# Block 0 of a four-layer transformer kernel: whole V chunks, x tile 1 in halves, its transposes moved among the third chunk's products, x tile 3 loaded ahead of x tile 2

## The chip, the core and the metric

The kernel runs on one core of a Trainium2 chip. The metric is the device time of one execution in microseconds (us). Five engines work side by side: TensorE (PE, matrix products and transposes), VectorE (DVE), ScalarE (ACT), GpSimd (POOL) and SyncE (SP). Here SP only issues DMAs. ACT issues a few DMAs at the very start and then computes.

## The reference

Four layers are applied in turn to `x` of shape 1 x 2048 x 1024 (bf16). Each adds its result to `x`:

```
x = x + A(layernorm(x));  x = x + B(layernorm(x));  x = x + A(layernorm(x));  x = x + B(layernorm(x))
A: qkv = x @ wqkv; 32 heads of 32; each position attends to itself and 7 earlier positions, 2 apart;
   softmax over the 8 logits; weighted sum of v; @ wo
B: (relu(x @ W_gate) * (x @ W_up)) @ W_down        # 1024 -> 3584 -> 1024
```

The layernorm has no weights: it subtracts the row's mean and divides by the square root of the variance plus 1e-5.

## The kernel before

The 2048 positions are four blocks of 512, and each block is four tiles of 128 positions (`x_tiles[0]` to `x_tiles[3]` are block 0). All of `x` stays on the chip; weights stream through a ring of five slabs (`wring`), each of at most 1 MB.

The order on an engine is fixed when the program is built. `sp_dma` chains the DMAs that SP issues, `dv` chains VectorE's instructions, `pe_group` TensorE's, and `on("a", ...)` and `on("g", ...)` ScalarE's and GpSimd's in block 0. An instruction that waits holds up everything behind it on its engine. DMAs use eight completion semaphores in rotation. A DMA waits at its issue until the DMA eight places earlier has landed.

The change touches the first products, the V projection of block 0. `w_v` is loaded as eight chunks of 128 rows of `wqkv` by 1024 columns (256 KB each), four to a slab; `load_slab` writes them out one by one, and halves some by columns. `kc` numbers the chunks. `v_first` multiplies them: `prod(kc, t)` is two products of 128x512, one for each half of the columns, of chunk `kc` with tile `t`, into accumulators that live until `kc` = 7. `head()` is the order on TensorE, written out by hand.

Before a tile can be multiplied, it must be centred (its mean subtracted) and turned (transposed). Tiles 0 and 1 are turned on TensorE when only centred; the division by the deviation comes later, on the results (`put`, on VectorE) and on the turned tiles (`widen`). `open_up()` starts tile 0: its halves' sums (`half_sums`, one on VectorE, one on ScalarE), `centre(0)`, `turn(0)` into four PSUM tiles, four copies back to SBUF by VectorE; then tile 1's mean in one pass of ScalarE (`act_mean(1)`) and `centre(1)`. Tile 1 is turned after the products of tile 0 with chunks 0 to 2. Its transposes lie in two PSUM tiles, which VectorE and ScalarE copy. Tiles 2 and 3 are divided too before they are turned (`apply`), tile 2 by TensorE (`later`) and tile 3 by a DMA transpose (`turn_last`). Their statistics, and those of tiles 0 and 1, are made on VectorE (`bn`, `aggr`), ScalarE (`square_of`, `act_mean`) and GpSimd (`power`) while TensorE multiplies chunks 3 to 7. `spread_rstd` turns the two deviations for `widen`. Tiles 2 and 3 are then multiplied with all eight chunks, and the q and k products of block 0 follow.

Ahead of this, ten products of constants (`scratch`) keep TensorE busy until `x` is there.

Of the kernel before, what the change touches and what calls it, by code (L numbers as in the profile page):

```python
# [36 lines left out]
def kernel(  # L37
# [86 lines left out]
    def sp_dma(dst, src, transpose=False):  # L124
        start = nc.sync.dma_start_transpose if transpose else nc.sync.dma_start
        if tail_sp[0] is None:
            tail_sp[0] = start(dst, src).ins  # L127
        else:
            with tc.issue_after(tail_sp[0]):
                tail_sp[0] = start(dst, src).ins  # L130
# [49 lines left out]
    def load_x(b, tiles=range(TPB)):  # L180
        for t in (b * TPB + i for i in tiles):
            if t == 0:
                sp_dma(x_tiles[t][:, 0:SLAB], x_dram[t * P:(t + 1) * P, 0:SLAB])
                nc.scalar.dma_start(x_tiles[t][:, SLAB:D], x_dram[t * P:(t + 1) * P, SLAB:D])
            elif t == 1:
                nc.scalar.dma_start(x_tiles[t][:], x_dram[t * P:(t + 1) * P, :])
            else:
                sp_dma(x_tiles[t][:], x_dram[t * P:(t + 1) * P, :])

# [36 lines left out]
    def want_down(n, half, at, gap):  # L226
        for s in range(NSL):
            rows = slice(8 * s, min(8 * (s + 1), FC))
            want(("d", n, half, s), wd_v[:, rows, half * SLAB:(half + 1) * SLAB], at + gap * min(8 * (s + 1), FC))

    def load_slab(key, src):
        shp = list(src.shape)
        t = wring.tile([P, 8 * SLAB], BF16, tag="slab", name="w_" + "_".join(str(k) for k in key))
        tv = t[:, 0:shp[1] * shp[2]].rearrange("p (a b) -> p a b", b=shp[2])
        if key[0] == "v0":
            for i in range(KC // 2):
                if (key[1], i) == (1, 0):
                    load_x(0, [2, 3])
                width = SLAB if (key[1], i) in ((0, 2), (1, 0)) else D
                for c in range(0, D, width):  # L240
                    sp_dma(tv[:, i:i + 1, c:c + width], src[:, i:i + 1, c:c + width])
        else:
            sp_dma(tv, src)
        slab[key] = tv
# [84 lines left out]
    def ln_first():  # L329
# [4 lines left out]
        def on(eng, f, *args, **kwargs):  # L334
            if eng == "v":
                dv(f, *args, **kwargs)
            elif eng in last:
                with tc.issue_after(last[eng]):
                    last[eng] = f(*args, **kwargs).ins
            else:  # L340
                last[eng] = f(*args, **kwargs).ins

        def small(name, bufs=4):
            return stat_pool.tile([P, 1], F32, tag="f" + name, name=name, bufs=bufs)
# [24 lines left out]

        parts = {}  # L370

        def half_sums():
            parts[0] = [small("part0"), small("part1")]
            on("v", nc.vector.tensor_scalar, xna[:, 0, 0:SLAB], x_tiles[0][:, 0:SLAB], 1.0 / D, None, op0=ALU.mult,
               op1=ALU.add, accum_out=parts[0][0][:])
            on("a", nc.scalar.activation, xna[:, 0, SLAB:D], x_tiles[0][:, SLAB:D], ACT.Identity, scale=1.0 / D,
               accum_out=parts[0][1][:])

        def centre(t):
            for h in range(2):  # L380
                cols = slice(h * SLAB, (h + 1) * SLAB)
                if t == 0:
                    on("v", nc.vector.tensor_scalar, xna[:, t, cols], x_tiles[t][:, cols], parts[t][0][:],
                       parts[t][1][:], op0=ALU.subtract, op1=ALU.subtract)
                else:
                    on("v", nc.vector.tensor_scalar, xna[:, t, cols], x_tiles[t][:, cols], mean[t], None,
                       op0=ALU.subtract)

        def square_of(src, t):
            sq = small("sq1")  # L390
# [3 lines left out]
        def act_mean(t):  # L394
            mn = small("mean1")
            on("a", nc.scalar.activation, xna[:, t, :], x_tiles[t][:], ACT.Identity, scale=1.0 / D, accum_out=mn[:])
            mean[t] = mn[:]
# [29 lines left out]
        def turn(t, halves=(0, 1)):  # L427
            if t in tps:
                pass
            elif t == 0:  # L430
                tps[t] = [psum.tile([P, KC // 4, P], BF16, tag="acc", name=f"tp{h}")[:] for h in range(4)]
            else:
                tps[t] = [pool["turns"].tile([P, KC // 2, P], BF16, tag=f"half{h}", name=f"tp{h}")[:] for h in range(2)]
            for c in (h * (KC // 2) + i for h in halves for i in range(KC // 2)):
                n = KC // len(tps[t])
                with pe_group():
                    tail_pe[0] = nc.tensor.transpose(tps[t][c // n][:, c % n, :], xna[:, t, c * P:(c + 1) * P],  # L437
                                                     ident[:]).ins

        def copy(t, eng, h, parts=1):  # L440
            f = nc.vector.tensor_copy if eng == "v" else nc.scalar.copy
            n = KC // len(tps[t])
            m = n // parts
            for i in range(0, n, m):
                on(eng, f, hold["xnT"][:, t, h * n + i:h * n + i + m, :], tps[t][h][:, i:i + m, :])

        def open_up():
            warm = small("warm")
            on("a", nc.scalar.activation, warm[:], one(1), ACT.Identity)
            scratch([BLK] * 9 + [BLK // 2])  # L450
            half_sums()
            centre(0)
            turn(0)
            for h in range(4):
                copy(0, "v", h)
            act_mean(1)
            centre(1)

        hold.update(on=on, bn=bn, aggr=aggr, apply=apply, turn=turn, copy=copy, widen=widen,
# [27 lines left out]
    def v_first(ln):  # L487
        st = att[0]
        accs = {}

        def prod(kc, t, hs=(0, 1)):
            for h in hs:
                if kc == 0:
                    accs[t, h] = psum.tile([P, SLAB], F32, tag="acc", name="acc_v")
                with pe_group():
                    mm(accs[t, h][:], lhsT=ln["xnT"][:, t, kc, :],
                       rhs=slab["v0", kc // (KC // 2)][:, kc % (KC // 2), h * SLAB:(h + 1) * SLAB],
                       start=(kc == 0), stop=(kc == KC - 1))

        def put(t):  # L500
            for h in range(2):
                v = ln["xn"][:, t, h * SLAB:(h + 1) * SLAB]
                if t < 2:
                    dv(nc.vector.tensor_scalar, v, accs.pop((t, h))[:], ln["rpair"][:, t:t + 1], None, op0=ALU.mult)
                else:
                    ln["on"]("a", nc.scalar.copy, v, accs.pop((t, h))[:])

        def later(t, h):
            ln["turn"](t, (h,))
            ln["copy"](t, "a", h, 2 - h)  # L510

        def turn_last():
            sp_dma(ln["xnT"][:, TPB - 1, :, :], ln["xn"][:, TPB - 1, :], True)
            load_x(1, [1])

        def head():
            ln["open_up"]()
            for kc in range(3):
                prod(kc, 0)
            ln["turn"](1)  # L520
            ln["copy"](1, "v", 0)
            ln["copy"](1, "a", 1)
            prod(3, 0)
            for kc in range(4):
                prod(kc, 1)
            for h in range(2):
                for t in range(2):
                    prod(4, t, (h,))
            for t in range(2):
                prod(5, t)  # L530
            ln["bn"](2, 0)
            ln["bn"](2, 1)
            ln["aggr"](2)
            sq = ln["square_of"](x_tiles[3][:], 3)
            ln["act_mean"](3)
            ln["bn"](1, 0)
            ln["apply"](2)
            ln["act_power"](3, sq)
            ln["power"](0, ln["square_of"](ln["xn"][:, 0, :], 0)[:], 1.0)
            ln["bn"](1, 1)  # L540
            ln["apply"](3)
            ln["aggr"](1)
            turn_last()
            prod(6, 0)
            prod(6, 1)
            later(2, 0)
            prod(7, 0)
            put(0)
            later(2, 1)
            prod(7, 1)  # L550
            ln["spread_rstd"]()
            put(1)
            ln["widen"]()
            for t in range(2, TPB):
                for kc in range(KC):
                    prod(kc, t)
                put(t)
            tail_act[0] = ln["last"]["a"]

        return head  # L560
# [482 lines left out]
    for t, steps in enumerate(norm_at):  # L1043
        ev.extend(zip(steps, (stats[t], apply[t], turn(t))))
    spread([turn_v(t) for t in range(TPB)], t_qk0 + 19.0, 0.01)
    spread([store_v_first(c0, c1) for c0, c1 in ((0, 3), (3, 6), (6, 8))], t_qk1 + 3.4, 0.87)
    ev.append((t_qk0 + 18.0, lambda: load_x(3)))
    spread(qk_steps(0, ln_a[0], "qk01"), t_qk0, GRP)
    spread(prod_sum_steps(0), t_sum0, 4.4)
# [146 lines left out]
```

## Time and profile before

| | |
|---|---|
| median of 3 runs | 1614.24 us (1614.2 to 1614.36) |
| the profiled execution | 1614.92 us, of which span 1613.2 us |
| PE busy | 1606.4 us (100% of the span), 7444 products recorded |
| DVE, ACT, POOL busy | 1140.9, 477.3, 183.3 us |
| granted TensorE clock | 1.00 |

The span runs from the first to the last instruction that the profiler recorded; the 1.7 us between it and the execution's time lie outside. Busy time counts a product from its start to its modelled end, and the ends overlap: in a dense stretch 128x512 products start 0.216 us apart though each is shown with 0.38 us. So idle time is better read from starts than from the busy share.

When the weights and tiles of block 0 landed, from the semaphore records of the trace (the last of the 16 counts of each DMA; us from the span's start):

| DMA | issued | landed |
|---|---|---|
| tile 0, two halves (SP and ACT) | 0.81, 0.80 | 3.66, 3.49 |
| tile 1 (ACT) | 1.24 | 5.16 |
| chunks 0, 1 | 1.27, 1.75 | 5.35, 6.70 |
| chunk 2, two halves | 2.23, 2.71 | 7.09, 7.45 |
| chunk 3 | 3.19 | 8.13 |
| tiles 2, 3 | 3.66, 4.16 | 8.81, 9.51 |
| chunk 4, two halves | 5.18, 5.55 | 9.86, 10.19 |
| chunks 5, 6, 7 | 6.72, 7.11, 7.57 | 10.85, 11.49, 12.89 |

### The profile page before, as it was taken

The page shows a single profiled execution, that of the slowest core. Times are in us where ns is not written, and L with a number is a line of the kernel's source. Part 1 is how long each engine was busy: PE and PEld are TensorE (multiplying, and loading weights), DVE is VectorE, ACT ScalarE, POOL GpSimd, SP SyncE. Part 2 cuts the span into 40 slices and gives each one's busy share as a digit, 9 for nine tenths or more (in the row PEclk, how much of TensorE's full clock was granted, in tenths as well). Part 3 has the DMA queues.
Part 4 walks back from the last instruction along what each step waited for, and adds up shares of the span by engine and source line. Part 5 has one row for each costly group of instructions (what it writes and reads, how often), then busy time and mean ns, then how long its engine had stood idle before and what let it go on. Part 6 is the DMA issues. An engine that isn't in the chain of part 4 may idle for free.

```text
span 1613.2 us, 18644 instructions
## 1 busy us (share of the span) xinstructions
PE 1606.4 (100%) x7444; PEld 776.2 (48%) x7494; DVE 1140.9 (71%) x967; ACT 477.3 (30%) x976; POOL 183.3 (11%) x172
## 2 busy tenths in 40 slices
PE   9999999999999999999999999999999999999999
PEld 5646544444444445444454444544445444444444
DVE  7999979997989698929389393993939939311211
ACT  4952311131125313603136031361313311131110
POOL 3500000010002002300053000530005100000000
DMA  9897867596669666784747857488575885655452
GB/s 287 214 215 251 212 177 239 188 231 199 201 195 239 184 189 198 203 241 147 231 153 206 232 159 230 151 205 249 164 227 156 203 244 157 209 168 171 157 164 71
DMA packets 365015, 319.22 MB, mean 198 GB/s; under 512 B 110592, under 2 KB 339456, under 8 KB 364416
## 3 DMA queue, kind: packets, MB, share of 16 engines
q1 hardware_dynamic: 364352, 317.41, 67.7%
q8 instruction: 58, 0.95, 0.2%
q10 hardware_dynamic: 576, 0.62, 0.1%
q14 instruction: 29, 0.24, 0.0%
HBM read 266.29 MB, written 34.66 MB: 187 GB/s over the span
## 4 chain that ended last, share of the span: by engine, by line
PE 99%; DMA 0%; issue 0%; SPq 0%; DVE 0%
PE acc_u L141 24%; PE acc_g L141 24%; PE dacc L141 18%; PE acc_k L141 7%; PE acc_q L141 7%; PE acc_v L141 7%; PE acc_wo L141 7%; PE dacc_pair L141 6%; DMA w_v<-in_A_wqkv_dram 0%; PE tp L437 0%; PE L L141 0%; SPq L130 0%; SPq L127 0%; DVE x L947 0%
## 5 line engine op out<-in xcount | busy, mean ns | idle before, releaser
L141 PE MATMUL acc_g<-xnT_b,w_g 128*128 128x512 bf16 x1792 | 423.5, 379 | 0.0
L141 PE MATMUL acc_u<-xnT_b,w_u 128*128 128x512 bf16 x1792 | 423.4, 379 | 0.0
L895 ACT ACTIVATE r<-acc_g 128x512 bf16<-128x512 f32 x224 | 133.6, 596 | 727.7 <-PE acc_g L141 690.9
L115 DVE TENSOR_TENSOR hT<-acc_u,r 128x512 bf16<-128x512 f32 x224 | 150.7, 686 | 240.9 <-PE acc_u L141 238.2
L141 PE MATMUL dacc<-w_d,hT 128*128 128x512 bf16 (+1 forms) x1372 | 301.9, 376 | 1.5
L141 PEld LDWEIGHTS <-hT 128*128 128x128 bf16 x1820 | 176.6, 98 | 210.5
L141 PEld LDWEIGHTS <-w_u 128*128 128x128 bf16 x1792 | 175.0, 98 | 211.8
L141 PEld LDWEIGHTS <-w_g 128*128 128x128 bf16 x1792 | 175.0, 98 | 211.7
L115 DVE TENSOR_TENSOR pv<-a,vhm 128x4096 bf16<-128x4096 bf16 x64 | 143.5, 2283 | 0.0
L947 DVE TENSOR_TENSOR x<-dacc,x 128x512 bf16<-128x512 f32 (+1 forms) x38 | 24.7, 677 | 154.0 <-PE dacc L141 154.0
L708 DVE TENSOR_TENSOR t<-q,k 128x2048 f32<-128x2048 bf16 x56 | 128.0, 2292 | 6.7 <-ACT k L644 4.6
L115 DVE TENSOR_TENSOR t<-q,k 128x2048 f32<-128x2048 bf16 x56 | 127.3, 2284 | 0.9
L649 POOL COPY kh<-k 128x14 bf16<-128x14 bf16 x40 | 58.5, 1471 | 503.1 <-ACT k L644 503.1
L115 DVE TENSOR_TENSOR pv<-pv 128x1024 bf16<-128x1024 bf16 (+1 forms) x128 | 113.7, 949 | 0.0
L141 PE MATMUL acc_wo<-w_o,oT 128*128 128x512 bf16 x498 | 111.1, 379 | 0.7
L724 DVE TENSOR_TENSOR ac<-ac,t 128x2048 f32<-128x2048 f32 x48 | 109.7, 2284 | 0.3
L115 DVE TENSOR_TENSOR ac<-ac,t 128x2048 f32<-128x2048 f32 x48 | 109.6, 2283 | 0.0
L276 POOL TENSOR_TENSOR st_b<-st_b,neg_half 128x1 f32<-128x1 f32 x29 | 41.4, 1434 | 528.6 <-ACT st_b L275 528.6
L141 PE MATMUL dacc_pair<-w_d,hT 128*128 128x512 bf16 (+1 forms) x413 | 94.0, 376 | 0.4
L141 PEld LDWEIGHTS <-oT 128*128 128x128 bf16 x512 | 50.0, 98 | 60.4
L271 ACT ACTIVATE xn_b<-x 128x1024 bf16<-128x1024 bf16 x29 | 30.3, 1045 | 131.6 <-DVE x L115 69.5
L482 ACT CAST vT<-acc_v 128x512 bf16<-128x512 f32 x56 | 32.6, 583 | 55.0 <-PE acc_v L141 54.1
(143 smaller groups left out, 1228.1 us busy)
## 6 DMA issues: line engine op xcount, KB each, us to landing
w_g<-in_B_W_gate_dram SPq DMA_DIRECT2D x56, 1024.0 KB, 7.0
w_u<-in_B_W_up_dram SPq DMA_DIRECT2D x56, 1024.0 KB, 5.4
w_d<-in_B_W_down_dram SPq DMA_DIRECT2D x48, 1024.0 KB, 6.3
w_o<-in_A_wo_dram SPq DMA_DIRECT2D x16, 1024.0 KB, 7.9
vhm<-v_d SPq DMA_DIRECT2D x32, 284.0 KB, 6.8
oT<-o_d SPq DMA_DIRECT2D x32, 256.0 KB, 3.5
w_d<-in_B_W_down_dram SPq DMA_DIRECT2D x16, 512.0 KB, 3.7
v_d<-vT SPq DMA_DIRECT2D x7, 1024.0 KB, 10.2
```

Of the source, the lines that this page charges most:

```text
L115: tail_dve[0] = f(*args, **kwargs).ins
L141: tail_pe[0] = nc.tensor.matmul(*args, **kwargs).ins
L271: nc.scalar.activation(xn, xt[:], ACT.Square, accum_out=sq)
L276: nc.gpsimd.tensor_tensor(rstd, vpe, neg_half[:, 0:1], op=ALU.pow)
L482: tail_act[0] = nc.scalar.copy(st["vT"][:, c, :], acc[:]).ins
L649: nc.gpsimd.tensor_copy(khalo[n][:, c, :], k[:, BLK:BLK + HALO])
L708: nc.vector.tensor_tensor(t[:], i0, i1, op=ALU.mult)
L724: nc.vector.tensor_tensor(o, i0, i1, op=ALU.add)
L895: tail_act[0] = nc.scalar.activation(rs[j][:], acc[:], ACT.Relu).ins
L947: run = dv if n < NB - 2 else (lambda f, *args, **kwargs: f(*args, **kwargs))
```

## The change

1. Chunks 2 and 4 are loaded whole, in one DMA each instead of two. Tile 1 is loaded in two DMAs of 512 columns, both issued by ACT.
2. On SP tile 3 is loaded ahead of chunk 3 and tile 2 ahead of chunk 4; before, both stood ahead of chunk 4, tile 2 first.
3. Tile 1's sum is made on ScalarE in two halves (`half_sums(1)`) instead of one pass, and `centre` subtracts both parts as for tile 0. Of tile 0's four copies the last two move from VectorE to ScalarE.
4. On TensorE tile 1's eight transposes no longer stand in one piece after chunk 2's products of tile 0: four stand ahead of each of these two products. Chunks 0 to 2 are multiplied with tile 1 next, and only then chunk 3 with tile 0.
5. Behind that VectorE makes the statistics of tile 1 ahead of tile 2's instead of between and after the `apply` steps, and `spread_rstd` stands ahead of `put(0)`.
6. The store of block 0's V, 50 us later, is four DMAs of two column groups instead of three (3, 3 and 2). With one DMA more here, one more for tile 1 and two fewer for the chunks, the rotation of the semaphores behind it is as before.

Beyond these, each engine has the same instructions in the same order.

```diff
             elif t == 1:
-                nc.scalar.dma_start(x_tiles[t][:], x_dram[t * P:(t + 1) * P, :])
+                for c in range(0, D, SLAB):
+                    nc.scalar.dma_start(x_tiles[t][:, c:c + SLAB], x_dram[t * P:(t + 1) * P, c:c + SLAB])
...
+    late_x = {(0, 3): 3, (1, 0): 2}
...
             for i in range(KC // 2):
-                if (key[1], i) == (1, 0):
-                    load_x(0, [2, 3])
-                width = SLAB if (key[1], i) in ((0, 2), (1, 0)) else D
-                for c in range(0, D, width):
-                    sp_dma(tv[:, i:i + 1, c:c + width], src[:, i:i + 1, c:c + width])
+                if (key[1], i) in late_x:
+                    load_x(0, [late_x[key[1], i]])
+                sp_dma(tv[:, i:i + 1, :], src[:, i:i + 1, :])
...
-        def half_sums():
-            parts[0] = [small("part0"), small("part1")]
...
+        def half_sums(t):
+            parts[t] = [small("part0"), small("part1")]
+            for h in range(2):
+                cols = slice(h * SLAB, (h + 1) * SLAB)
+                if (t, h) == (0, 0):
+                    on("v", nc.vector.tensor_scalar, xna[:, t, cols], x_tiles[t][:, cols], 1.0 / D, None,
+                       op0=ALU.mult, op1=ALU.add, accum_out=parts[t][h][:])
+                else:
+                    on("a", nc.scalar.activation, xna[:, t, cols], x_tiles[t][:, cols], ACT.Identity, scale=1.0 / D,
+                       accum_out=parts[t][h][:])
...
-            half_sums()
+            half_sums(0)
             centre(0)
             turn(0)
+            half_sums(1)
             for h in range(4):
-                copy(0, "v", h)
-            act_mean(1)
+                copy(0, "v" if h < 2 else "a", h)
             centre(1)
...
             ln["open_up"]()
+            for kc in range(2):
+                prod(kc, 0)
+            for h in range(2):
+                ln["turn"](1, (h,))
+                ln["copy"](1, "va"[h], h)
+                prod(2, 0, (h,))
             for kc in range(3):
-                prod(kc, 0)
-            ln["turn"](1)
-            ln["copy"](1, "v", 0)
-            ln["copy"](1, "a", 1)
-            prod(3, 0)
-            for kc in range(4):
                 prod(kc, 1)
-            for h in range(2):
+            for kc in range(3, 6):
                 for t in range(2):
-                    prod(4, t, (h,))
-            for t in range(2):
-                prod(5, t)
+                    prod(kc, t)
+            ln["bn"](1, 0)
+            ln["bn"](1, 1)
+            ln["aggr"](1)
             ln["bn"](2, 0)
...
-            ln["bn"](1, 0)
-            ln["apply"](2)
             ln["act_power"](3, sq)
             ln["power"](0, ln["square_of"](ln["xn"][:, 0, :], 0)[:], 1.0)
-            ln["bn"](1, 1)
+            ln["apply"](2)
             ln["apply"](3)
-            ln["aggr"](1)
+            ln["spread_rstd"]()
             turn_last()
...
-            ln["spread_rstd"]()
             put(1)
...
-    spread([store_v_first(c0, c1) for c0, c1 in ((0, 3), (3, 6), (6, 8))], t_qk1 + 3.4, 0.87)
+    spread([store_v_first(c0, c1) for c0, c1 in ((0, 2), (2, 4), (4, 6), (6, 8))], t_qk1 + 3.4, 0.87)
```

More of the change, by code (lines that the diff above doesn't have):

```diff
@@ L370, in ln_first @@
         parts = {}
-        def half_sums():
-            parts[0] = [small("part0"), small("part1")]
[L374 to L377, printed above, removed]
+        def half_sums(t):
[8 more added lines that the diff above has]
+                       accum_out=parts[t][h][:])
         def centre(t):
@@ L381, in centre @@
                 cols = slice(h * SLAB, (h + 1) * SLAB)
[L382 to L387, printed above, removed]
+                on("v", nc.vector.tensor_scalar, xna[:, t, cols], x_tiles[t][:, cols], parts[t][0][:], parts[t][1][:],
+                   op0=ALU.subtract, op1=ALU.subtract)
         def square_of(src, t):
```

## The prediction

> **What bounds the kernel now.** I read the page first: the busy table and the chain that ended last.
>
> ```profile
> PE 1606.4 (100%) x7444; PEld 776.2 (48%) x7494; DVE 1140.9 (71%) x967; ACT 477.3 (30%) x976; POOL 183.3 (11%) x172
> PE 99%; DMA 0%; issue 0%; SPq 0%; DVE 0%
> ```
>
> TensorE carries the whole chain, so only time in which it does not start products can be won. I went through the starts of its records, product by product. Dense products of 128x512 start 0.216 us apart, transposes 0.056 us. Beyond that pitch there are 1.8 us in all, and from 8.17 us to the end only two gaps of 0.09 us (at 100 us). So the change acts on the first 8.17 us, or it makes a new gap. The chain of waits there, and TensorE's timeline:
>
> ```profile
> 1.75 4.95 DMA w_v<-in_A_wqkv_dram
> 6.70 0.04 issue
> 6.74 1.13 PE acc_v L141 x4
> 7.87 0.45 PE tp L437 x8
> 8.32 3.71 PE acc_v L141 x17
> ```
>
> ```profile
> 4.97 0.72 PE L437 MATMUL tp<-ident,xn_first 128*128 128x128 bf16 x8 [0.20 <-DVE xn_first L115]
> 5.64 0.61 PE L141 MATMUL acc_v<-w_v,xnT_first 128*128 128x512 bf16 x2
> 6.74 1.13 PE L141 MATMUL acc_v<-w_v,xnT_first 128*128 128x512 bf16 x4 [0.50 <-DMA w_v<-in_A_wqkv_dram]
> 7.71 0.61 PE L437 MATMUL tp<-ident,xn_first 128*128 128x128 bf16 x8
> 8.17 1.05 PE L141 MATMUL acc_v<-w_v,xnT_first 128*128 128x512 bf16 x4
> ```
>
> Product by product: chunk 0 starts at 5.64 and 5.865, so TensorE is free at 6.08. Chunk 1 lands at 6.70 and starts at 6.74: 0.66 lost (0.50 in the view, which counts modelled ends). Chunk 2's second half lands at 7.45 and starts at 7.494 instead of 7.387: 0.11 lost. Chunk 3 lands at 8.13 and starts at 8.171 instead of 8.155: 0.02. Thus 0.79 us are lost to landings, and from 8.17 on TensorE is dense. The measure of the change is when it becomes dense with the same work behind it: tile 0 times chunks 0 to 2 (6 products) and tile 1's eight transposes.
>
> **The landings.** The trace's packets take 46 ns for 1 KB and 84 ns for 2 KB on 16 engines. A 256 KB load in rows of 2 KB is 128 x 84 / 16 = 0.67 us, in two halves 256 x 46 / 16 = 0.74. Chunk 3 indeed landed 0.68 after chunk 2, and chunk 2's halves 0.39 and 0.36 apart. So a slab made whole saves 0.07, tile 1 in halves costs 0.07. Chunk 1, behind tile 1, lands at 6.70 + 0.07 = 6.77; chunk 2 whole at 7.45, as before.
>
> **Tile 1's path.** Before, on ScalarE:
>
> ```profile
> 1.72 1.28 ACT L341 ACT_TABLE_LOAD   x1 [1.72 <-PEq L1180]
> 3.51 0.63 ACT L339 ACTIVATE xn_first<-x 128x512 bf16<-128x512 bf16 x1 [0.30 <-DMA x<-in_A_x_dram]
> 5.19 1.06 ACT L339 ACTIVATE xn_first<-x 128x1024 bf16<-128x1024 bf16 x1 [0.95 <-DMA x<-in_A_x_dram]
> 6.15 0.19 ACT L339 ACTIVATION_READ_ACCUMULATOR xn_first<-x 128x1 f32 x1
> ```
>
> Its third DMA issue (0.45, as that of tile 1 at 1.24) pushes the table load and the warm-up to an end near 3.70, so tile 0's sum starts at 3.70 instead of 3.51 and is read out at 4.42. VectorE's own half is read at 4.38 and its centring started at 4.50, so this costs nothing; without that cover the first transposes come up to 0.2 later, and the 0.66 wait for chunk 1 takes that up. For tile 1: if the second half lands at T, its sum (0.63) and read-out (0.19, overlapping 0.09, as at 3.51) end at T + 0.75, VectorE starts 0.03 later, its first half takes 0.41 (the row of tile 0's two-part subtraction), and TensorE follows after 0.06: first four transposes at T + 1.25. Before, T was 5.16; with 0.07 for the small packets 5.23, so they are ready at 6.48, long before TensorE is through with chunk 1.
>
> **TensorE, step by step.** Chunk 1 at 6.81 and 7.03, free 7.25. Four transposes to 7.47. Chunk 2 lands 7.45, product at 7.49, free 7.71. Four transposes to 7.93, second product to 8.15. Tile 1's first PSUM tile is complete 0.16 after its last transpose's slot (7.63); VectorE's copy of 128x512 took 0.42, ready at 8.10. Its chunks 0 to 2 (six products) start at 8.15. In short: dense at the landing of chunk 2 plus 0.69, that is 8.14, against 8.17. The gap of 0.11 is filled by transposes, but chunk 2's second product ends no earlier; before, the transposes filled the wait for chunk 3, which is now not needed until 9.44. **Sum: -0.03 us.**
>
> **What comes behind.** Six products end at 9.44; chunk 3, now behind tile 3, lands near 8.81. Chunk 4 is wanted at 10.30. Ahead of it are the same bytes as before (both tiles, chunk 3), and it saves its halves: 10.19 - 0.07 = 10.12, a margin of 0.18. Chunks 5, 6, 7 are wanted at 11.17, 12.03 and 13.11 and land, at the landings of before, at 10.85, 11.49 and 12.89. Each DMA issue costs SP 0.43 to 0.48; none gets later, since the DMAs eight places ahead that they wait for are tile 0, tile 1 and chunks 0 to 2, landed by 7.45. SP's queue is two issues shorter until the stores.
>
> ScalarE's two copies from PSUM (0.37 each) stand behind tile 1's sums and end near 7.2; chunk 4 wants them at 10.30. VectorE: tile 1's statistics (2 x 0.68 + 0.21) from 8.1 to 9.7, tile 2's when it lands at 9.5, hence `apply(2)` at 11.9 and `apply(3)` at 12.5, against 11.31 and 12.97. TensorE turns tile 2 at 12.9, 0.5 after its `apply`, so the delay is covered (uncovered, it would cost up to 0.6). Tile 3's DMA transpose, which waits for `apply(3)`, is issued 0.5 earlier than at 13.54; the issues queued behind it on SP gain too. GpSimd's last deviation comes at 13.3 (before 14.8), so `put` and `widen` end near 19.5 instead of 20.0, ahead of the q products at 21.2. The accumulators that `put(0)` frees, now at 15.8 (before 15.4), are wanted at 17.7. The fourth store is one more issue on SP (0.4 to 1.0) where SP stood from 57.5 to 58.6 waiting for a copy of q.
>
> So all stays covered, and 1614.92 - 0.03 = 1614.89 for the profiled execution, or 1614.24 - 0.03 = 1614.2 for the median.
>
> **Rival 1, slower: the second half of tile 1 is late and its transposes hold up TensorE's queue.** Before, a late tile 1 delayed only work behind chunk 2; now its transposes stand ahead of chunk 2's products. By the path above it decides when T + 1.25 is past 7.25, T past 6.0. The row that bears on it, DMA queues from 3.5 to 4.0 us:
>
> ```profile
> q1 hardware_dynamic: 43, 0.09, 51.9%
> q10 hardware_dynamic: 43, 0.09, 45.1%
> ```
>
> Both queues (q1 SP's, q10 ACT's) moved the same number of packets. If that stays so with tile 1's packets halved, its 16 packets on an engine take 16 x (46 + 84) = 2.08 us instead of 8 x (84 + 84) = 1.34: T = 5.16 + 0.74 = 5.9, just in time. If it lands only with chunk 1, T = 6.7: transposes at 7.95, products 8.17 to 8.39 and 8.61 to 8.83, dense at 8.83, +0.66 us: 1614.9. Against it: tile 1 starts ahead of most of the chunks, and a longer share of chunk 1's packets brings chunk 1 earlier. [...]
>
> **Rival 2, faster: chunks land earlier than my packet count says.** The slowest of the 16 engines sets the landing: chunk 1's first count came at 5.45, its last at 6.70, since single packets there took 0.3 to 0.6 us instead of 0.084. With other packet sizes these delays can fall elsewhere. Dense is chunk 2's landing plus 0.69, so a landing at 7.05 gives -0.4: 1613.8. More isn't likely, since all landings to 8.8 us trail the first count by some 1.2 us and follow it steadily.
>
> **Rival 3, slower for real: TensorE falls back to its slow pace.** Until 4.2 us the constant products start 0.43 apart, twice the later pitch, and 0.66 us of waiting did not bring that back. If new waits did, a stretch like the first (3.4 us, 8 products at 0.215 extra) would cost 1.7 us, and two stretches 3.4: 1617.7. It decides from a wait clearly longer than 0.66, which only rival 1 could supply. [...]
>
> That the change does not do what it says is excluded by its instruction order, which has the transposes and loads where the text puts them.
>
> **The numbers.** Forecast as summed 0.66, rival 1 0.15, rival 2 0.14, rival 3 or a loss elsewhere 0.05. The range takes in rival 1's far end (1614.9) and reaches toward rival 2's (1613.7); a later stall of some us is left out. A measurement of this kernel can tell about 0.2%, 3.2 us, from no change; the first three cases all lie within it. Nothing can win 3.2 us, since the whole loss ahead of 8.17 us that landings cause is 0.79. Hence same 0.94, slower 0.05, faster 0.01.
>
> **What would show it.** Right: TensorE's products of chunk 1 near 6.8, transposes in two groups of four ahead of chunk 2's products, dense from about 8.15, no new gap behind 9.4, `apply(2)` later and tile 3's DMA transpose earlier. Wrong: transposes waiting for VectorE (rival 1), chunk 1 well ahead of 6.7 (rival 2), a gap at 10.3 for chunk 4, products 0.43 apart after 4.5 us (rival 3), or a gap anywhere past 20 us.

## Result and profile after

| | before | after |
|---|---|---|
| median | 1614.36 us (22 executions, 1614.06 to 1614.78) | 1616.42 us (22 executions, 1614.99 to 1618.71) |
| ratio | | 1.0013, 95% interval 1.0007 to 1.0019 |
| profiled execution | 1614.92 us, span 1613.2 | 1614.99 us, span 1613.3 |

The change costs 2.1 us. That is less than the 0.2% named in the prediction, but the interval excludes no change, and the time lies outside the forecast range of 1613.7 to 1614.9. The change in spread matters as much as the median: 0.7 us before, 3.7 us after. Four of the 22 executions of after have a granted clock of 0.999 over the whole span, and these are the four longest (1617.84 to 1618.71).

The traced execution of after is the fastest of the 22, and that of before is longer than all of its 22. They differ by only 0.07 us, so comparing these two traces hides the cost. What they do show is the place. First the page of after, busy line and chain:

```profile
PE 1609.2 (100%) x7494; PEld 777.3 (48%) x7494; DVE 1140.7 (71%) x965; ACT 477.9 (30%) x980; POOL 187.3 (12%) x172
PE 99%; DMA 0%; ACTq 0%; ACT 0%; DVE 0%; issue 0%
```

ACTq and ACT have entered the chain that ended last; before, neither was in it. The same chain of after in its first 14 us (start, duration, what):

```profile
1.23 0.45 ACTq L187
...
1.71 4.37 DMA x<-in_A_x_dram
...
6.10 0.73 ACT xn_first L340 x2
...
6.86 0.42 DVE xn_first L115
...
7.33 0.40 PE tp L438 x4
```

Line 187 is ACT's issue of tile 1. The second half of tile 1, issued at 1.71, lands at 6.08. Its sum, its centring and its transposes follow without slack, and TensorE stands in that line. Before, the link here was chunk 1 of `w_v`. TensorE's timeline of after:

```profile
5.71 1.33 PE L141 MATMUL acc_v<-w_v,xnT_first 128*128 128x512 bf16 x4
7.33 0.40 PE L438 MATMUL tp<-ident,xn_first 128*128 128x128 bf16 x4 [0.29 <-DVE xn_first L115]
7.56 0.38 PE L141 MATMUL acc_v<-w_v,xnT_first 128*128 128x512 bf16 x1
7.78 0.39 PE L438 MATMUL tp<-ident,xn_first 128*128 128x128 bf16 x4
8.00 1.71 PE L141 MATMUL acc_v<-w_v,xnT_first 128*128 128x512 bf16 x7
```

By starts, chunk 1's second product stands at 6.665 and the first transpose at 7.329, where 6.88 was possible (0.216 behind the product): 0.45 us are lost to the wait (0.29 in the view, which counts modelled ends). Tile 1's products are dense from 8.246, and the last product starts 0.06 us later than before. From 8.25 us on there is no new gap; the two gaps of 0.09 us near 100 us are there as before.

### The profile page after: what moved, and what is told of

Its sections match the earlier page's. It is cut to its first block, busy times and chain, and to the rows that moved or that the text cites. A ratio compares the mean times of both kernels' runs of the same rounds, so it can differ in the third digit from the quotient of the medians.

```text
span 1613.3 us, 18697 instructions
## 1 busy us (share of the span) xinstructions
PE 1609.2 (100%) x7494; PEld 777.3 (48%) x7494; DVE 1140.7 (71%) x965; ACT 477.9 (30%) x980; POOL 187.3 (12%) x172
## 4 chain that ended last, share of the span: by engine, by line
PE 99%; DMA 0%; ACTq 0%; ACT 0%; DVE 0%; issue 0%
PE acc_u L141 24%; PE acc_g L141 24%; PE dacc L141 18%; PE acc_k L141 7%; PE acc_wo L141 7%; PE acc_q L141 7%; PE acc_v L141 7%; PE dacc_pair L141 6%; DMA x<-in_A_x_dram 0%; PE tp L438 0%; ACT xn_first L340 0%; PE L L141 0%; ACTq L187 0%; DVE xn_first L115 0%; ACTq L184 0%; DVE x L946 0%
```

## Experiments

Every execution was compared with executions of the kernel before on the same chip; those medians were 1614.30 to 1614.65. T is the landing of tile 1's second half in the trace (last of 16 counts).

### The changed kernel again, on three more chips

Edit: none.

> The changed kernel as it is, for a second trace and for the spread of its executions. Theory L (tile 1's second half lands late by an amount that differs between executions, and its transposes, now ahead of chunk 2's products, hold up TensorE): times again between 1615 and 1619, and in the trace the wait ahead of the first group of four transposes is as long as the landing of the second half is past 6.0 us. Theory S (something later, in the stores or the rotation of semaphores, stalls now and then): a new gap past 20 us. Theory C (TensorE's slow pace): products 0.43 us apart somewhere behind 4.5 us.

> The changed kernel as it is, on the same chip, for the comparison and for a third trace. As before: 1615 to 1620, with the granted clock at 0.999 or 0.998 in the executions above 1617 and 1.000 below. Should the traced execution be one of the slow ones: products 0.43 us apart behind the first transposes.

> The changed kernel as it is. Theory: on a chip on which some executions show a clock below 1.000, these are at 1617 to 1620 us and the rest at 1615 to 1616.5 us; on a chip without them all are at 1615 to 1616.5 us. Rival (the long executions are a long wait at full pace): long executions with a clock of 1.000.

Measured: 1617.61 us (ratio 1.0022, 1.0013 to 1.0030), 1615.34 (1.0005, 0.9996 to 1.0014) and 1615.82 (1.0008, 0.9999 to 1.0017). On the first chip 6 of 11 executions had a clock of 0.998 or 0.999; on the others none had, and none took more than 1616.53 us. The chain of the first of these runs, traced in an execution of 1615.96 us:

```profile
1.74 5.32 DMA x<-in_A_x_dram
...
7.07 0.73 ACT xn_first L340 x2
...
8.30 0.40 PE tp L438 x4
```

It is the same chain, with a landing 0.97 us later and a time 0.97 us longer. The four traced executions together:

| T | chunk 1 landed | first transpose | execution | execution minus T |
|---|---|---|---|---|
| 6.08 | 6.41 | 7.33 | 1614.99 | 1608.91 |
| 6.27 | 6.47 | 7.52 | 1615.18 | 1608.91 |
| 6.64 | 6.83 | 7.89 | 1615.56 | 1608.92 |
| 7.05 | 6.85 | 8.30 | 1615.96 | 1608.91 |

In all four, at full clock, the time of the changed kernel is T + 1608.91 us: the first transpose comes at T + 1.25, and all behind it is fixed. By this the median of the result, 1616.42, had T near 7.5 (an estimate, beyond the traced range). In these four the half lands within 0.4 us of chunk 1. Which of the two lands first goes with a few hundredths of a us at the issue: in the first three ACT issues the half 0.03 us ahead of SP's chunk 1, and the half lands first; in the fourth SP is ahead by 0.01, and chunk 1 lands first. In four other kernels below that load tile 1 in the same way (the halves alone, the order alone, and the two traces of the filled kernel) SP is ahead by 0.01 as well, and the half lands 0.2 to 0.5 us behind chunk 1.

### An ordinary execution of before

Edit: none to the kernel before.

> The kernel before, for a trace of an ordinary execution: the one that the prediction was made from was 0.6 us above the median. If the landings of its first chunks were its ill luck, chunk 1 lands near 6.0 here and TensorE is dense near 7.5 instead of 8.17. If not, dense is again near 8.17 and the 0.6 us lie elsewhere.

Measured: 1614.36 us (1614.09 to 1614.72); traced at 1614.5. Its chain over the first 14 us:

```profile
by line: PE acc_v L141 51.8%; PE scratch L141 30.1%; PE tp L437 13.2%; issue 0.7%
...
0.84 4.21 PE scratch L141 x10
5.05 0.95 PE tp L437 x8
6.01 1.44 PE acc_v L141 x6
7.45 0.45 PE tp L437 x8
7.89 3.71 PE acc_v L141 x17
```

No DMA is in it, and TensorE is dense from 7.73 (by starts), not from 8.17. Chunk 1 landed at 6.09, not 6.70, before TensorE was through with chunk 0, whose products were still at the slow pace (0.41 us apart, until 6.2). So the 0.79 us "lost to landings" that the prediction started from belong to the one execution that it read; this one has no landing to win back.

### Tile 1 whole again

```diff
-                for c in range(0, D, SLAB):
-                    nc.scalar.dma_start(x_tiles[t][:, c:c + SLAB], x_dram[t * P:(t + 1) * P, c:c + SLAB])
+                nc.scalar.dma_start(x_tiles[t][:], x_dram[t * P:(t + 1) * P, :])
```

> The changed kernel with tile 1 loaded in one DMA again, all else as changed. Theory L with the halves as its cause: tile 1 lands near 5.2 us, both half sums end near 6.6, the transposes are ready by 7.1, dense near 8.15; median 1614.2 to 1614.6 and a spread of at most 0.8 us. If the loads of tiles 2 and 3, the whole chunks, or the four stores are the cause: median stays near 1616.4 with the wide spread.

Measured: 1614.80 us (1614.65 to 1615.40), ratio 1.0003 (0.9994 to 1.0012), all clocks 1.000. That is 0.2 us more than was expected, and 2.8 less than the changed kernel beside it (1617.61). With the same edit and the sum in one pass (`centre(1)` then subtracts one mean), by this further edit,

```diff
-            half_sums(1)
+            act_mean(1)
```

> The changed kernel with tile 1 loaded whole and its sum made in one pass again; what is left of the change are the order on TensorE, the loads of tiles 2 and 3, the whole chunks and the stores. Theory L with tile 1's path as the whole cause: transposes ready 0.25 us earlier than with the two half sums, at about 6.7, so the 0.5 us by which the whole tile with half sums stood above the kernel before go to 0.2 or less: 1614.2 to 1614.6. If the rest of the change costs by itself: 1614.7 or more.

Measured: 1614.64 (1614.54 to 1615.00) against 1614.52 before, ratio 1.0001 (0.9992 to 1.0010). The median lies between the two values that were to decide, but the difference from the kernel before beside it is only 0.12 us. Two views, ScalarE's timeline of the first kernel and TensorE's of the second:

```profile
5.12 0.63 ACT L339 ACTIVATE xn_first<-x 128x512 bf16<-128x512 bf16 x1 [0.89 <-DMA x<-in_A_x_dram]
5.75 0.61 ACT L339 ACTIVATE xn_first<-x 128x512 bf16<-128x512 bf16 x1
```

```profile
5.86 1.46 PE L141 MATMUL acc_v<-w_v,xnT_first 128*128 128x512 bf16 x4
7.15 0.39 PE L441 MATMUL tp<-ident,xn_first 128*128 128x128 bf16 x4
```

Whole, tile 1 lands at 5.10 (first kernel) and 4.89 (second). In the first kernel the two half sums still run one behind the other and the transposes come at 6.96; in the second nothing waits between chunk 1's products and the transposes. So the load in halves is most of the cost. The two half sums may add some tenths (0.50 us against the kernel before beside it with them, 0.12 without, on two chips). The rest of the change taken together (transposes ahead, whole chunks, tile 3 first, the order on VectorE, the fourth store) costs nothing that this can resolve.

### The halves alone, and the order alone

In the kernel before, the load of tile 1 in two DMAs and nothing else:

```diff
-                nc.scalar.dma_start(x_tiles[t][:], x_dram[t * P:(t + 1) * P, :])
+                for c in range(0, D, SLAB):
+                    nc.scalar.dma_start(x_tiles[t][:, c:c + SLAB], x_dram[t * P:(t + 1) * P, c:c + SLAB])
```

> The kernel before with nothing changed but tile 1 loaded in two DMAs on ACT's queue (its sum is still one pass, which waits for both). Theory L with the halves as its cause: the late landing appears here too, but the transposes stand behind chunk 2's products and the one-pass sum is 0.3 us longer, so median 1615 to 1616.5 with a spread of 2 us or more. If the order of TensorE is needed for the loss: 1614.3 with the narrow spread of before.

Measured: 1615.89 us (1615.53 to 1616.40), ratio 1.0009 (1.0000 to 1.0018). T is 6.42, chunk 1 6.21; the one-pass sum ends at 7.56 and the transposes, which here stand behind chunk 2's products, start at 8.10 after a wait of 0.93. So the late half costs 1.6 us without any change of order. The spread that was expected did not come: 0.9 us, all clocks 1.000.

In the changed kernel, the transposes back behind chunk 2's products:

```diff
-            for kc in range(2):
+            for kc in range(3):
                 prod(kc, 0)
             for h in range(2):
                 ln["turn"](1, (h,))
                 ln["copy"](1, "va"[h], h)
-                prod(2, 0, (h,))
```

> The changed kernel with tile 1's eight transposes again in one piece behind chunk 2's products with tile 0, all else as changed. Theory L: the same late landing, but TensorE has two products (0.43 us) more to do ahead of it, so the loss shrinks by at most 0.43 us: median near 1616.0, wide spread. If the new place of the transposes alone is the cause: 1614.3 and a narrow spread.

Measured: 1615.94 us (1615.31 to 1618.77), ratio 1.0012 (1.0004 to 1.0021); two of 11 executions at clock 0.999. T is 7.00, chunk 1 6.46, the transposes at 8.25. With T this late, it is T + 1.25 that decides in the traced execution, wherever the two products of chunk 2 stand. The changed kernel beside it took 1617.61 us, with 6 of 11 below a clock of 1.000; at full clock it took 1615.63 to 1617.13, this one 1615.31 to 1616.69. So most of the difference in the medians is the number of executions with a lowered clock. Ahead of the transposes TensorE's wait is shorter here by the two products (0.43 us).

### Why the half is late

Both halves on SP, ahead of chunk 0:

```diff
-                    nc.scalar.dma_start(x_tiles[t][:, c:c + SLAB], x_dram[t * P:(t + 1) * P, c:c + SLAB])
+                    sp_dma(x_tiles[t][:, c:c + SLAB], x_dram[t * P:(t + 1) * P, c:c + SLAB])
```

> The changed kernel with both halves of tile 1 issued by SP ahead of chunk 0 instead of by ACT. If turn taking between two queues makes the second half late, in one queue it lands in its place, ahead of chunk 0 at about 4.9 us, chunks 0 and 1 as late as before; median 1614.2 to 1615.0, spread at most 0.8 us. If small packets or the third issue as such make it late, the median stays above 1615.5 with the wide spread.

Measured: 1615.28 us (1614.82 to 1616.97), ratio 1.0006 (0.9997 to 1.0015), higher and wider than was expected. The halves land at 3.91 and 5.13, but chunk 0 only at 6.01 and chunk 4 at 10.42, so TensorE waits 0.51 and 0.28 us for those.

The halves stay on ACT, as its first two DMAs; tile 0's second half goes to SP:

```diff
-                nc.scalar.dma_start(x_tiles[t][:, SLAB:D], x_dram[t * P:(t + 1) * P, SLAB:D])
+                sp_dma(x_tiles[t][:, SLAB:D], x_dram[t * P:(t + 1) * P, SLAB:D])
```

> The changed kernel with tile 0's second half issued by SP, so that tile 1's halves are ACT's first two DMAs and each is issued 0.45 us earlier; chunks 0 and 1 are issued 0.48 us later. Theory I (the second half is late because its issue is third in ACT's queue, at the same time as chunk 1's, and then lands with chunk 1): it now lands near 4.5, well ahead of chunk 1; median 1614.4 to 1615.2, spread at most 1 us. Theory T (half-size packets in turn with the larger ones make it late): it still lands within 0.4 us of chunk 1, and the wide spread stays, median above 1615.5.

Measured: 1615.03 us (1614.72 to 1615.44), ratio 1.0003 (0.9995 to 1.0012). ScalarE's timeline:

```profile
4.25 0.63 ACT L340 ACTIVATE xn_first<-x 128x512 bf16<-128x512 bf16 x1 [1.01 <-DMA x<-in_A_x_dram]
4.88 0.61 ACT L340 ACTIVATE xn_first<-x 128x512 bf16<-128x512 bf16 x1
5.49 0.61 ACT L340 ACTIVATE xn_first<-x 128x512 bf16<-128x512 bf16 x1
```

The wait in the first line is for tile 0's half; tile 1's two sums follow without one. The second half has the same size and packets and the same queue, but T is 4.41 and ScalarE is never short of it. Chunk 1 still lands at 6.61. So neither the small packets nor ACT's queue makes it late: its place among the issues does. As ACT's third DMA it is issued at 1.71, behind chunk 0 (1.27) and beside chunk 1 (1.744), and it lands with chunk 1. The moment alone does not decide: with both halves on SP the second was issued at 1.74 too, ahead of chunks 0 and 1, and landed at 5.13. This edit moves both sides, the half 0.47 us forward and the two chunks 0.46 back.

### A longer wait, and TensorE's slow pace

The second half is issued by SP behind chunk 2, 3 or 4, which makes the wait longer and leaves the rest as it is (here behind chunk 2; `(0, 3)` and `(1, 0)` for the others):

```diff
-                for c in range(0, D, SLAB):
-                    nc.scalar.dma_start(x_tiles[t][:, c:c + SLAB], x_dram[t * P:(t + 1) * P, c:c + SLAB])
+                nc.scalar.dma_start(x_tiles[t][:, 0:SLAB], x_dram[t * P:(t + 1) * P, 0:SLAB])
...
                 sp_dma(tv[:, i:i + 1, :], src[:, i:i + 1, :])
+                if (key[1], i) == (0, 2):
+                    sp_dma(x_tiles[1][:, SLAB:D], x_dram[P:2 * P, SLAB:D])
```

> The changed kernel with tile 1's second half issued by SP behind chunk 2 instead of by ACT, so that it lands late in every execution: near 7.4 us, transposes 1.25 us later at 8.65, dense near 9.5. Theory L alone: the loss against the kernel before is the wait, about 1.5 to 2 us, median near 1616.0, with a narrow spread and no slow products. With the slow pace of TensorE as a second step (theory C, the granted clock below 1 in the slow executions): some executions show products 0.43 us apart behind the wait and take 1.7 us more.

> The same with the half issued behind chunk 3: landing near 8.6 us, transposes at 9.9, dense near 10.7. Theory L alone: median near 1617.3, narrow spread, granted clock 1.000 to three places. Theory C: the wait of some 2.7 us brings TensorE's slow pace back in most executions, products 0.43 us apart for about 3.4 us, granted clock 0.999 or less, median 1618.5 to 1620.5.

> The changed kernel with tile 1's second half issued by SP behind chunk 4: landing near 10.2 us, TensorE without work from 7.0 to about 11.5, longer than behind chunk 3. Theory C (TensorE's pace halves after a long wait, and how long is a matter of where the wait falls): now in nearly every execution, the traced one too: products behind the wait 0.43 us apart, granted clock 0.998, median 1621 to 1623, made of a wait of 4.5 us and slow products worth 2 to 3 us. If the extra 3 us behind chunk 3 were a second late landing instead: products 0.216 us apart, clock 1.000, median near 1619 and single executions 3 us above.

> The same kernel without the constants, beside it on the same chip: 1620.6 to 1621.5 us and clock 0.998 as before, by the theory; by the rival the same.

| half issued behind | wait in the trace (by starts) | median (range) | executions with clock below 1.000 |
|---|---|---|---|
| chunk 2 | 1.77 us | 1615.79 (1615.64 to 1618.29) | 1 of 10, the longest |
| chunk 3 | 3.08 us | 1620.34 (1617.52 to 1620.68) | 3 of 5, the longest |
| chunk 4 | 4.07 us | 1621.20 (1620.57 to 1621.47) | 4 of 4 |
| chunk 4, again | 4.45 us | 1621.37 (1620.30 to 1621.97) | 5 of 5 |

The stretches of the first kernel behind chunk 4 (window, busy and products, granted clock, DMA share, GB/s):

```profile
7.00:9.90 2.90, 0.15 (x1) 1.00 1.05 397
10.00:11.00 1.00, 0.00 (x0) 0.50 1.06 387
11.00:13.30 2.30, 2.25 (x12) 0.50 1.04 389
13.30:16.70 3.40, 3.40 (x10) 0.50 0.27 98
16.80:20.00 3.20, 3.20 (x19) 1.00 0.52 92
```

TensorE idles from 7 to 11 us; during the wait the granted clock falls to 0.50, and it stays there until 16.77, for 6.83 us in the clock records. Work resumes at 11.05 with products 0.43 apart, the prediction's rival 3. The fall comes well before the wait is over: TensorE's last product ends at 7.15, and the clock falls at 9.94 in the clock records. In the second run behind chunk 4 the last product ends at 6.74 and the clock falls at 8.73, after 2.0 us. Its stretches, in the same columns:

```profile
6.50:7.50 1.00, 0.24 (x2) 1.00 1.05 404
7.50:9.90 2.40, 0.00 (x0) 0.76 1.05 396
9.90:11.00 1.10, 0.00 (x0) 0.50 1.03 372
```

The length of 6.83 us also sets the scale of the clock column: half of it, 3.41 us at 0.50, in a span of 1615 would be a mean of 0.9989, shown as 0.999, and the whole is 0.9979, shown as 0.998 for both traces. By that, at most 1.7 and 3.4 us are lost (an estimate). In the first run of the changed kernel above the executions at 0.999 took 1617.6 to 1618.6 us and those at 0.998 some 1620.1, against 1615.6 to 1617.1 at 1.000.

Now with products of constants in the wait (sixteen, twelve for chunk 3 and six for the changed kernel itself); they use an accumulator that the first product of tile 1 overwrites:

```diff
-                if kc == 0:
+                if kc == 0 and (t, h) not in accs:
...
+            accs[1, 0] = psum.tile([P, SLAB], F32, tag="acc", name="acc_v")
+            for _ in range(16):
+                with pe_group():
+                    mm(accs[1, 0][:], lhsT=one(P), rhs=one(BLK), start=True, stop=True)
             for h in range(2):
                 ln["turn"](1, (h,))
```

> The half of tile 1 is issued behind chunk 4, as in the run with a wait of 4.07 us, and 16 products of constants (3.46 us of TensorE at 0.216) stand between chunk 1's products and the transposes. Theory (a wait of this length brings TensorE's slow pace back, and that costs 2.9 us beyond the wait): about 0.6 us of waiting is left, no product behind it at 0.43 us, clock 1.000 in every execution, time about 1618.4 to 1618.8 us, 2.5 to 3 us below the same kernel without the constants. Rival (the length is the wait alone): as without them, 1621 us.

Measured: 1619.02 us (1618.55 to 1620.73), all seven at clock 1.000, against 1621.37 on the same chip without the constants. That is 0.2 us above the expected range, and what made the longest so long is open. TensorE's timeline and two of the stretches from above:

```profile
6.73 3.66 PE L141 MATMUL acc_v<-const-bfloat16-1.0 128*128 128x512 bf16 x16
10.87 0.40 PE L439 MATMUL tp<-ident,xn_first 128*128 128x128 bf16 x4 [0.48 <-DVE xn_first L115]
```

```profile
10.00:11.00 1.00, 0.52 (x5) 1.00 1.05 395
13.30:16.70 3.40, 3.40 (x19) 1.00 0.27 97
```

The transposes come at 10.87, little earlier than the 11.05 and 11.03 without the constants, yet 2.35 us are won: 19 products are recorded from 13.3 to 16.7 where there were 10 in the first kernel without them. So the wait behind chunk 4 cost its length and, at 4.07 and 4.45 us, the slow pace as well; with the constants in it the clock stayed at 1.000 in all seven executions.

> The kernel with the half behind chunk 3, and 12 products of constants (2.6 us) on TensorE between chunk 1's products and the first transposes; their sums are overwritten by tile 1's first products and change nothing. The landing stays as late, near 8.4 us. Theory C: TensorE is not idle for long, its pace stays, and the slow executions vanish: 1617.4 to 1618.2 in all, clock 1.000. If the slow executions come from a later landing or from something downstream: most executions again above 1620.

Measured: 1617.66 us (1617.21 to 1618.34), all 11 at clock 1.000. The kernel without constants ran on another chip, so this agrees but is no test side by side.

> The changed kernel with 6 products of constants (1.3 us) between chunk 1's products and the first transposes; tile 1's first products overwrite their sums. If TensorE's slow pace makes the upper part of the spread: the clock reads 1.000 in all or nearly all executions, none is above 1617.5, and the fastest are up to 0.8 us slower than the changed kernel's fastest, since the constants end near 8.3. If the upper part is later landings alone: executions above 1618 stay.

> The changed kernel with six products of constants between chunk 1's products and tile 1's transposes. Theory: no execution below a clock of 1.000, all within 1615.7 to 1616.5 us, also where the changed kernel itself has executions at 1617 to 1620 us. Rival: the same long executions as without the constants.

Measured: 1615.95 us and 1616.03 us, against 1615.34 and 1615.82 for the changed kernel beside them. This did not settle it: on these two chips no execution of the changed kernel was slowed, and the filled one had one of 22 at clock 0.999 (1618.58), where none was expected.

## Why the prediction was wrong

**The step that failed: "with 0.07 for the small packets 5.23".** T was 6.08 to 7.05 in the traces. The prediction knew that the second half is ACT's third DMA and issued 0.45 us later; it used this for the table load, but priced the half by its bytes alone, as if it were issued where tile 1 was. Issued behind chunk 0 and beside chunk 1, it lands with chunk 1. When the same half was issued as ACT's second DMA, with the chunks behind it, it landed at 4.41. This is rival 1 at its far end ("if it lands only with chunk 1"), which was given 0.15, and in part beyond it (T was 6.7 there). Of the price for packets sharing the queues, T = 5.9: no trace is that early; T came 0.2 to 1.2 later. That count has both queues move as many packets. In the trace of after they moved 133 (SP's) and 138 (ACT's) from 4 to 5 us, and 15 of the half's 16 counts had come by 5.30, but the last came at 6.08.

**The step from T to TensorE was right:** the first transposes come at T + 1.25 in all four traces.

**The base was mis-sized.** The sum was made against an execution at 1614.92 us with 0.79 us lost to landings; the median execution is 0.6 us shorter, and the one traced of that kind has no landing in its chain. Rival 1's +0.66 us was worked out against that long execution but set on the median, as 1614.9. On the execution that it belongs to it gives 1615.58, and T + 1608.91 gives 1615.61 for its T of 6.7: the price was right and the base wrong. Against 1614.36 the loss at full clock was 0.5 to 2.8 us (1614.86 to 1617.13 in 45 executions of the changed kernel).

**Rival 3 was set too far off.** Its price fits the clock column: one stretch of 3.4 us (the length of the first in the trace of before), 1.7; two, 3.4. Its own condition, a wait clearly longer than 0.66 us that only rival 1 could supply, came true. How long a wait brings the slow pace back was shown by no run when its chance was set. Executions with a lowered clock came in kernels whose traced wait was 1.77 us (1 of 10), 3.08 (3 of 5) and over 4 (9 of 9). In the two traces that show the fall it came 2.8 and 2.0 us behind the end of the last product (9.94 behind 7.15, 8.73 behind 6.74). In both it came 3.4 us behind the beginning of the fast pace (6.53 and 5.31), and the clock stayed at 0.50 for 6.83 us. In the trace behind chunk 3 the wait lasts 2.92 us (6.91 to 9.83, by the last product's end), and the clock stays at 1.00. So the length of the wait alone did not decide: 2.92 us passed without a fall, and 2.0 and 2.8 were enough for one. What decides beside it was not shown.

The slowed executions behind chunks 2 and 3 need not have waited longer than the others of their kernel: less 1.7 us (1618.29 behind chunk 2) and less 2.9 (1620.34 to 1620.68 behind chunk 3; half of the 5.7 us that the kernel behind chunk 4 worked at 0.50) they come to 1616.6 and 1617.4 to 1617.8, near what the others took (to 1616.66, and 1617.52 and 1617.99). Of 55 executions of the changed kernel 10 had a clock below 1.000, of 132 of the kernel before beside the experiments none. By T + 1608.91, the longest at full clock, 1617.13, had T near 8.2 and so a wait of some 2.1 us (an estimate: 8.22 + 1.25 - 7.33, the last being where TensorE was through with chunk 1 in the trace with T = 7.05). That lies among the waits at which slowed executions appear.

**Left open:** no slowed execution of the changed kernel itself was traced. That the slow pace makes them rests on the clock column, whose two steps fit one and two stretches, and on the kernels with longer waits. What began the slowed execution of the filled kernel isn't known, nor why the landing is so much later on some chips and in some executions.

**What held:** chunk 4 landed at 9.72 and was multiplied at 10.41, with no stall; `apply(2)` started at 11.87 and `apply(3)` at 12.49 (11.9 and 12.5 were forecast); tile 3's DMA transpose was issued 0.5 us earlier (13.07) than in the profiled execution of before, though not than in the ordinary one (12.87); no gap past 9.4 us is new. Rival 2, chunks landing earlier, came true in part (chunk 1 at 6.41 in the trace of after, but at 6.09 in the ordinary execution of before) and was worth nothing, since TensorE then waited for tile 1.

No version tried beats the kernel before. The one with tile 1 whole and its sum in one pass equals it within what can be resolved. The likely reason is that an ordinary execution has no wait for a landing in its chain that this change could fill.

## What to carry to other kernels

Price a load that is split by what has been issued ahead of its last piece and beside it, on all queues, not by its own bytes (here T was 6.08 to 7.05 where the bytes gave 5.23). Before moving an instruction forward in an in-order queue, ask for the latest landing that its input has over many executions, since a wait placed ahead of ready work can turn a late landing into time one for one (here T + 1608.91 us in four traces). Compare the traced execution with the list of times first: a trace from the slow end of before shows losses that the median has not, and one from the fast end of after hides what the change costs.

## What was not expected of the hardware

- The same DMA of 128 KB, issued at 1.70 to 1.74 us, landed at 6.08, 6.27, 6.64 and 7.05 us in four executions.
- The full clock pace of TensorE began at different times: in one execution of before products were 0.41 us apart until 6.2 us, in the profiled one they were already 0.22 apart at 5.64.
- The granted clock fell to 0.50 only 2.0 and 2.8 us behind the end of TensorE's last product, stayed there for 6.83 us, and in the second case held through 5.7 us of dense work behind the wait.
